# A fused GFNet and GEGLU kernel: the first piece of the forward matrix issued from ScalarE's DMA queue

## Chip, cores and metric

The kernel runs on 1 core of one Trainium2 chip. The metric is the device time in microseconds (us) of one execution. The runs of the kernel before lie between 456.63 and 457.2 us, with a median of 457.14 us over 3 runs.

## What is computed

The input x has 2048 rows of 512 numbers, all float32. The first half of the reference normalises each row, takes a two-dimensional real FFT, multiplies by complex weights, transforms back and adds x. The second half normalises the result again and runs a gated feed-forward layer with 1376 hidden columns, and adds its input.

```python
X = rfft2(layernorm(x));  X = X * (w_r + 1j * w_i);  h = x + irfft2(X)
n = layernorm(h)
g = n @ w_gate;  u = n @ w_up
h2 = h + (gelu(g) * u) @ w_down
```

## The kernel before, in words

**Tiling.** The FFTs are written as matrix products with cosine and sine tables, in stages. The 2048 rows are held as 128 partitions times 16 blocks: `gh[:, b]` is block b of x (128 x 512), and the forward matrix `mfs` holds for each block b a 128 x 128 piece `mfs[:, b]`. The prediction is about the first stage, the transform over the rows, which takes the first 33 of some 455 us. The stages behind it are the transform over the columns with the filter (lines 411 to 482), the way back, and the feed-forward layer with its products split in three (line 96) for precision, which is most of the span.

**One block of the first stage.** For each block b:

- VectorE (DVE) takes mean and variance: `stats` (line 220) and `merge` (line 223). For blocks 5, 7, 9, 11 and 13 ScalarE (ACT) does that instead: `mean` (line 228) and `square` (line 233).
- `root` (line 240) takes 1/sqrt on ACT, with line 241 beside it on DVE, and `newton` (lines 246 to 248) refines it on DVE. The result is `rs[:, b]`.
- `fold` (lines 262 and 263) is on GpSimd (POOL): sums and differences of the two halves of a row, written to `pn`. `fold2` (lines 275 to 277) is a second difference on DVE, written to `uv`.
- `scale` (line 256) on ACT multiplies `mfs[:, b]` by `rs[:, b]` and writes `ms`. So a block needs its piece of the forward matrix here and nowhere else, and the layernorm's scale is folded into the matrix.
- `transform` (line 288) is the product on TensorE (PE) of `pn` and `uv` with `ms`; `keep` (line 293) moves the result from PSUM to `ts` on ACT.

From block 2 on blocks go in pairs (`GROUPS`, line 28), except the last two. Lines 298 to 398 write the order of all these steps out by hand; each engine executes its own instructions strictly in that order, so an instruction that waits holds up everything behind it on its engine.

**Loads.** All DMAs of the kernel before are issued from SyncE (SP), in the order of the code. `load_x` (line 182) loads blocks of x, `load_m` (line 179) pieces of the forward matrix:

```python
act.activation(m4[:, :1], eps, AF.Abs_reciprocal_sqrt)   # L184: loads ACT's table early
load_x(0, 1)
load_x(1, 2)
load_m(0, 2)      # the line that changes: 128 KB
load_x(2, 4)
load_x(4, 6)
load_m(2, 8)
```

A load of one block of x is 256 KB, of two blocks 512 KB. Behind these come the rest of x, the rest of the matrix, small tables (line 196), and weights (lines 131, 132, 202 and on). Completion of the DMAs is counted on eight semaphores that the loads take in turn, so the ninth load of the program waits at issue for the first one to land, the tenth for the second, and so on.

Of the kernel before, what the change touches and what calls it, by code (L numbers as in the profile page):

```python
# [57 lines left out]
def kernel(  # L58
# [15 lines left out]
    nc = tc.nc  # L74
# [87 lines left out]
    with (  # L162
# [8 lines left out]
        mfs = w1.tile([P, NB, P], F32, name="mfs", bufs=1)  # L171
# [6 lines left out]
        def load_m(b0, b1):  # L178
            nc.sync.dma_start(mfs[:, b0:b1], mf[:, b0:b1])

        def load_x(b0, b1):
            nc.sync.dma_start(gh[:, b0:b1], x3[:, b0:b1])
# [1 line left out]
        act.activation(m4[:, :1], eps, AF.Abs_reciprocal_sqrt)  # L184
        load_x(0, 1)
        load_x(1, 2)
        load_m(0, 2)
        load_x(2, 4)
        load_x(4, 6)
        load_m(2, 8)  # L190
# [965 lines left out]
```

## Time and profile before

| what | value |
|---|---|
| runs of the kernel before, median (lowest to highest) | 457.14 us (456.63 to 457.2), 3 runs |
| the profiled execution's own time | 456.41 us |
| span of its trace, first to last instruction | 454.6 us |
| time outside the span | 1.81 us |
| busy share of PE, DVE, ACT, POOL | 97%, 61%, 45%, 61% |
| DMA: moved in the span | 41.05 MB |

Every timestamp below counts from the first instruction of the span. A row of the timeline gives start, duration, engine, line, operation, what is written and read, how many instructions are merged in the row, and in brackets the idle time of the engine ahead of it and what ended it. SPq is SyncE's queue of DMA issues: the duration of its row is that of the issue, and the data land later. PEld is the loading of weights into TensorE.

### The profile page before, as it was taken

To read this page: it belongs to the slowest core of one execution; us is meant where nothing else is said; L and a number is where in the kernel's file an instruction comes from. 1 tells how busy PE (TensorE), PEld (TensorE's weight loads), DVE (VectorE), ACT (ScalarE), POOL (GpSimd) and SP (SyncE) were. 2 spreads that over 40 slices of the span, in tenths; PEclk is the share of its full clock that TensorE was granted. 3 is DMA by queue.
4 is the path that set the end of the run, shared out by engine and by line. 5 is a ranking of instruction groups with operands and counts; after the bars stand their busy time and mean duration, and the time that the engine had idled before them with its cause. 6 is when DMAs were issued, how large, how long until landed. Compare 5 with 4: busy or idle time off the path is not lost.

```text
span 454.6 us, 6435 instructions
## 1 busy us (share of the span) xinstructions
PE 438.9 (97%) x2289; PEld 371.4 (82%) x2289; DVE 276.9 (61%) x513; ACT 206.6 (45%) x433; POOL 275.5 (61%) x305
## 2 busy tenths in 40 slices
PE   3999998999999999999999999999999999999997
PEld 3899998788967777887888888888888888888876
DVE  5966986797665676358744579256565355535453
ACT  3979876688751233024422776242243024302420
POOL 5985996968868578828752744155566536663210
PEclk9999999999999999999999999999999999999999
DMA  8994804300031122112210203131022102210013
GB/s 253 399 406 132 284 32 156 123 25 1 25 115 47 48 92 92 48 47 71 69 46 25 70 25 128 57 85 55 25 70 69 48 24 71 69 46 25 23 66 121
DMA packets 21168, 41.05 MB, mean 90 GB/s; under 512 B 2064, under 2 KB 7696, under 8 KB 21008
## 3 DMA queue, kind: packets, MB, share of 16 engines
q1 hardware_dynamic: 21136, 40.64, 26.2%
q8 instruction: 18, 0.29, 0.3%
q14 instruction: 14, 0.11, 0.1%
HBM read 36.44 MB, written 4.19 MB: 89 GB/s over the span
## 4 chain that ended last, share of the span: by engine, by line
PE 89%; ACT 4%; DVE 2%; DMA 2%; issue 1%; SPq 1%; DVEq 0%; ACTq 0%
PE ps L747 26%; PE ps L100 15%; PE ps L102 15%; PE ps L101 15%; PE ps L416 3%; PE ps L515 3%; PE ps L427 3%; PE ps L448 2%; PE ps L288 2%; DMA gh<-in_x 2%; PE ps L848 1%; PE ps L956 1%; PE ps L554 1%; ACT ts L293 1%; PE ps L548 1%
## 5 line engine op out<-in xcount | busy, mean ns | idle before, releaser
L100 PE MATMUL ps<-cb,gu 128*128 128x512 f32 (+1 forms) x336 | 127.8, 380 | 2.0 <-ACT s L651 1.6
L747 PE MATMUL ps<-wd,a 128*128 128x512 f32 (+1 forms) x537 | 126.1, 388 | 0.2 <-DVE gh L750 0.2
L102 PE MATMUL ps<-cb,gu 128*128 128x512 f32 (+1 forms) x336 | 124.9, 372 | 0.0
L101 PE MATMUL ps<-cb,gu 128*128 128x512 f32 (+1 forms) x336 | 124.8, 371 | 0.0
L747 PEld LDWEIGHTS ps<-wd,a 128*128 128x128 f32 x537 | 99.2, 188 | 22.4 <-DVE gh L957 0.9
L156 POOL TENSOR_TENSOR gu<-raw,gu 128x768 fp32r<-128x768 f32 (+1 forms) x54 | 78.2, 1476 | 40.0 <-DVE gu L153 38.7
L651 ACT ACTIVATE s<-ps 128x512 f32<-128x512 f32 (+1 forms) x72 | 40.4, 561 | 134.4 <-PE ps L102 134.2
L100 PEld LDWEIGHTS ps<-cb,gu 128*128 128x128 f32 x336 | 63.2, 188 | 15.0 <-ACT s L651 2.2
L101 PEld LDWEIGHTS ps<-cb,gu 128*128 128x128 f32 x336 | 63.2, 188 | 11.7 <-issue 1.0
L102 PEld LDWEIGHTS ps<-cb,gu 128*128 128x128 f32 x336 | 63.2, 188 | 11.1
L753 DVE TENSOR_TENSOR gh<-ps,gh 128x512 f32<-128x512 f32 x48 | 33.0, 690 | 53.5 <-PE ps L747 53.4
L496 POOL TENSOR_TENSOR wd<-wdr,wd 128x512 fp32r<-128x512 f32 x22 | 28.5, 1295 | 51.5 <-ACT wd L494 51.5
L660 DVE TENSOR_TENSOR ps<-ps,s 128x512 f32<-128x512 f32 (+1 forms) x48 | 31.0, 649 | 24.8 <-PE ps L102 22.5
L666 ACT ACTIVATE a<-ps 128x512 fp32r<-128x512 f32 (+1 forms) x48 | 26.9, 561 | 39.0 <-DVE ps L660 38.6
L673 DVE TENSOR_TENSOR a<-ps,a 128x512 fp32r<-128x512 f32 (+1 forms) x48 | 30.7, 640 | 11.8 <-ACT a L666 10.4
L138 POOL TENSOR_TENSOR raw<-raw 128x256 f32<-128x256 f32 x20 | 14.7, 737 | 37.8 <-DMA raw<-in_wgu 36.7
L654 DVE TENSOR_TENSOR s<-ps,s 128x512 f32<-128x512 f32 (+1 forms) x48 | 30.8, 642 | 10.3 <-PE ps L102 8.7
L657 ACT ACTIVATE s<-s 128x512 f32<-128x512 f32 (+1 forms) x48 | 28.2, 592 | 18.4 <-DVE s L654 18.4
L654 DVE TENSOR_TENSOR ps<-ps,s 128x512 f32<-128x512 f32 (+1 forms) x24 | 15.7, 654 | 27.7 <-ACT s L651 27.7
L288 PE MATMUL ps<-ms,pn 128*128 128x128 f32 x120 | 17.6, 297 | 8.3 <-ACT ms L256 8.1
L288 PEld LDWEIGHTS ps<-ms,pn 128*128 128x128 f32 x120 | 16.1, 210 | 8.8 <-POOL pn L263 8.8
L153 DVE CAST gu<-raw 128x1792 fp32r<-128x1792 f32 x18 | 19.6, 1091 | 4.5 <-PE ps L101 2.9
(124 smaller groups left out, 609.7 us busy)
## 6 DMA issues: line engine op xcount, KB each, us to landing
raw<-in_wgu SPq DMA_DIRECT2D x40, 256.0 KB, 3.1
wt<-in_w SPq DMA_DIRECT2D x16, 520.0 KB, 5.4
wdr<-in_wd SPq DMA_DIRECT2D x22, 256.0 KB, 2.6
out<-gh SPq DMA_DIRECT2D x15, 256.0 KB, 2.0
gh<-in_x SPq DMA_DIRECT2D x7, 512.0 KB, 9.6
row<-in_x SPq DMA_DIRECT2D x12, 256.0 KB, 3.0
mis<-in_mi SPq DMA_DIRECT2D x1, 1024.0 KB, 10.7
a<-in_x SPq DMA_DIRECT2D x4, 256.0 KB, 4.3
```

The lines of the kernel that those rows point to most:

```text
L100: pe.matmul(o, lh, rh, start=(i == 0 and not onto), stop=False, skip_group_check=True)
L101: pe.matmul(o, lh, rl, start=False, stop=False, skip_group_check=True)
L102: last = pe.matmul(o, ll, rh, start=False, stop=(i == n - 1), skip_group_check=True)
L156: pooled["lo"] = pool.tensor_tensor(r[:, 1, m], t[:, m], r[:, 0, m].bitcast(F32), op=ALU.subtract)
L288: pe.matmul(pt[:, c], o, mc, start=(z == 0), stop=(z == len(parts[b][c]) - 1))
L496: pool.tensor_tensor(r[:, 1], t, r[:, 0].bitcast(F32), op=ALU.subtract)
L651: return lambda: act.activation(to, a, AF.Copy)
L654: return lambda: dve.tensor_tensor(to, a, b, op=ALU.add)
L660: return lambda: dve.tensor_tensor(u, u, g, op=ALU.mult)
L673: dve.tensor_tensor(a[:, 1], u, a[:, 0].bitcast(F32), op=ALU.subtract)
L747: pe.matmul(o, parts_of[tiles.index((q, f))][:, ha, i // 4, r], wds[f][:, hw, c], start=start, stop=stop)
L753: dve.tensor_tensor(gh[:, b, c], o, gh[:, b, c], op=ALU.add)
```

## The change

One line is replaced. The 128 KB piece of the forward matrix for blocks 0 and 1 is issued by ScalarE instead of SyncE. All other loads stay on SyncE in their order.

```diff
         act.activation(m4[:, :1], eps, AF.Abs_reciprocal_sqrt)
         load_x(0, 1)
         load_x(1, 2)
-        load_m(0, 2)
+        nc.scalar.dma_start(mfs[:, :2], mf[:, :2])
         load_x(2, 4)
         load_x(4, 6)
         load_m(2, 8)
```

On SyncE the first loads of the program stood as follows before; `gh` is x, `mfs` the forward matrix, and L196 loads the first small table.

```order
L182 DMA gh<-in_x 128x512 x2
L179 DMA mfs<-in_mf 128x256
L182 DMA gh<-in_x 128x1024 x2
L179 DMA mfs<-in_mf 128x768
L182 DMA gh<-in_x 128x1024 x2
L179 DMA mfs<-in_mf 128x1024
L182 DMA gh<-in_x 128x1024 x3
L196 DMA dfs<-in_df 128x520
```

And on SyncE in the changed program:

```order
L182 DMA gh<-in_x 128x512 x2
L182 DMA gh<-in_x 128x1024 x2
L179 DMA mfs<-in_mf 128x768
L182 DMA gh<-in_x 128x1024 x2
L179 DMA mfs<-in_mf 128x1024
L182 DMA gh<-in_x 128x1024 x3
L196 DMA dfs<-in_df 128x520
```

The row of 128x256 is gone, and every load behind it stands one place further ahead.

On ScalarE the changed program begins with these rows; `m` is the scrap output of the first activation, `ms` the scaled matrix, `jk` a scrap output of the statistics.

```order
L187 DMA mfs<-in_mf 128x256
L184 ACT_TABLE_LOAD
L184 ACTIVATE m_98<-eps 128x1
L240 ACTIVATE rs<-mv,eps 128x1
L256 ACTIVATE ms<-mfs,rs 128x128
L240 ACTIVATE rs<-mv,eps 128x1
L256 ACTIVATE ms<-mfs,rs 128x128
L228 ACTIVATE jk,m_98<-gh 128x512
```

The first row is new; the seven others stood there before in this order. The DMA stands ahead of the table load and of the first activation, though the code has it behind that activation. TensorE, VectorE and GpSimd have the same rows as before.

## Prediction

> **What bounds the kernel now.** I read the page first.
>
> ```profile
> span 454.6 us, 6435 instructions
> PE 438.9 (97%) x2289; PEld 371.4 (82%) x2289; DVE 276.9 (61%) x513; ACT 206.6 (45%) x433; POOL 275.5 (61%) x305
> ```
>
> TensorE is busy for 97% of the span, so the kernel is TensorE's work plus whatever keeps TensorE from beginning it. A load at the front can only change the second part. So next I read the chain of work that ended last, in order of time, for the first 30 us.
>
> ```profile
> 1.63 0.42 SPq L179
> 2.10 0.43 SPq L182
> ...
> 3.52 8.86 DMA gh<-in_x
> 12.38 0.02 issue
> 12.40 0.03 ACT jk L228
> ...
> 22.10 0.14 issue
> 22.23 7.83 PE ps L288 x68
> ```
>
> Three stretches follow each other: SyncE's issues, one load of x (blocks 6 and 7) that takes 8.86 us from issue to landing, and ScalarE's work, until TensorE takes over at 22.23 us and keeps the chain. The matrix piece that the change moves is in this chain only as an issue of 0.42 us at 1.63; its data are not in it. Now the timelines of the engines, ScalarE first.
>
> ```profile
> 0.73 1.28 ACT L184 ACT_TABLE_LOAD   x1 [0.73 <-PEq L1147]
> 2.02 0.20 ACT L184 ACTIVATE m<-eps 128x1 f32<-128x1 f32 x1
> 4.46 0.29 ACT L240 ACTIVATE rs<-mv,eps 128x1 f32<-128x1 f32 x1 [2.24 <-DVE mv L223]
> 6.75 0.40 ACT L256 ACTIVATE ms<-mfs,rs 128x128 f32<-128x128 f32 x1 [1.99 <-DMA mfs<-in_mf]
> 7.06 0.28 ACT L240 ACTIVATE rs<-mv,eps 128x1 f32<-128x1 f32 x1
> 7.96 0.40 ACT L256 ACTIVATE ms<-mfs,rs 128x128 f32<-128x128 f32 x1 [0.63 <-DVE rs L248]
> 9.94 0.63 ACT L228 ACTIVATE jk<-gh 128x512 f32<-128x512 f32 x1 [1.58 <-DMA gh<-in_x]
> ...
> 12.40 0.63 ACT L228 ACTIVATE jk<-gh 128x512 f32<-128x512 f32 x1 [0.22 <-DMA gh<-in_x]
> ```
>
> At 6.75 ScalarE has waited 1.99 us for the piece in question. But at 9.94 it waits again, 1.58 us, for blocks 4 and 5 of x, and at 12.40 another 0.22 us for blocks 6 and 7. GpSimd and TensorE:
>
> ```profile
> 5.62 0.72 POOL L263 TENSOR_TENSOR pn<-gh 128x256 f32<-128x256 f32 x1
> 8.28 1.27 POOL L262 TENSOR_TENSOR pn<-gh 128x512 f32<-128x512 f32 x1 [1.94 <-DMA gh<-in_x]
> ```
>
> ```profile
> 7.29 2.05 PE L288 MATMUL ps<-ms,pn 128*128 128x128 f32 x8 [7.29 <-ACT ms L256]
> ...
> 9.99 1.92 PE L288 MATMUL ps<-ms,pn 128*128 128x128 f32 x8
> 11.69 1.06 PE L288 MATMUL ps<-ms,uv 128*128 128x128 f32 x4
> 13.56 2.02 PE L288 MATMUL ps<-ms,pn 128*128 128x128 f32 x16 [0.80 <-ACT ms L256]
> ...
> 16.31 1.06 PE L288 MATMUL ps<-ms,pn 128*128 128x128 f32 x8
> 17.20 0.61 PE L288 MATMUL ps<-ms,uv 128*128 128x128 f32 x4
> ```
>
> GpSimd waits 1.94 us for blocks 2 and 3 of x, at 8.28. TensorE begins at 7.29 when the scaled matrix is there, does blocks 0 and 1, stops for 0.80 us and begins block 2 at 13.56. Weight loading shows who paces TensorE after that.
>
> ```profile
> 19.15 0.97 PEld L288 LDWEIGHTS ps<-ms,pn 128*128 128x128 f32 x8 [0.18 <-POOL pn L263]
> 22.20 0.97 PEld L288 LDWEIGHTS ps<-ms,pn 128*128 128x128 f32 x8 [0.30 <-POOL pn L263]
> ```
>
> So the front has two pacemakers of nearly the same length: GpSimd from 8.28 on, released by blocks 2 and 3, and ScalarE from 9.94 on, released by blocks 4 and 5 and once more by 6 and 7. The dense region moves only if **all these landings of x** move; blocks 0 and 1 are done in front of it and cost nothing when they end sooner.
>
> **The change, part by part.**
>
> *Matrix piece sooner.* Landing times by issue, in the first 30 us:
>
> ```profile
> gh<-in_x SPq DMA_DIRECT2D x2, 256.0 KB, 2.9
> mfs<-in_mf SPq DMA_DIRECT2D x1, 128.0 KB, 5.0
> ```
>
> Before, the piece is issued at 1.63 and lands 5.0 us later, at 6.63. After, its issue is ScalarE's first row, at about 0.73; with the 2.9 us of the first x loads it lands near 3.6, with its own 5.0 us near 5.7. The scale `rs` of block 0 decides then. DVE rows:
>
> ```profile
> 3.52 0.69 DVE L220 BATCH_NORM_STATS2 bn<-gh 128x6 f32<-128x512 f32 x1 [2.66 <-DMA gh<-in_x]
> 5.52 0.16 DVE L248 SCALAR_TENSOR_TENSOR rs<-ps,rs 128x1 f32<-128x1 f32 x1
> 7.37 0.16 DVE L246 SCALAR_TENSOR_TENSOR ps<-rs,ps 128x1 f32<-128x1 f32 x1 [0.75 <-ACT rs L240]
> ```
>
> It is ready at 5.52 + 0.16 = 5.68, so ScalarE scales at 5.7 to 6.1 instead of 6.75, and TensorE starts at 6.3 to 6.7 instead of 7.29. DVE's wait of 0.75 us at 7.37 mostly goes too, as ScalarE's second root is no longer held behind the scaling. What is late next is x: ScalarE's 1.58 us wait, GpSimd's 1.94 and TensorE's 0.80 simply grow. Worth **0** of the end.
>
> *One issue less on SyncE.* Blocks 2 and 3 are issued at 1.63 instead of 2.10, and each load behind them 2.10 - 1.63 = 0.47 us earlier. If their landings followed, the gain would be 0.47. But the same 128 KB still go through the same DMA engines, ahead of them or beside. How full these are:
>
> ```profile
> 1.50:2.00 0.50, 0.00 (x0) 0.00 (x0) 0.00 (x0) 0.50 (x1) 0.00 (x0) 1.00 0.40 66
> 2.00:2.50 0.50, 0.00 (x0) 0.00 (x0) 0.00 (x0) 0.22 (x2) 0.00 (x0) 1.00 0.83 250
> ...
> 3.00:3.50 0.50, 0.00 (x0) 0.00 (x0) 0.00 (x0) 0.00 (x0) 0.00 (x0) 1.00 0.97 363
> ...
> 9.00:9.50 0.50, 0.50 (x4) 0.50 (x4) 0.50 (x2) 0.00 (x0) 0.50 (x1) 1.00 1.06 285
> ...
> 11.50:12.00 0.50, 0.50 (x4) 0.50 (x4) 0.23 (x2) 0.50 (x3) 0.50 (x2) 1.00 1.08 442
> ```
>
> The last two columns are the DMA engines' share and GB/s. From 1.5 to 2.5 us they are free for (1 - 0.40) x 0.5 + (1 - 0.83) x 0.5 = 0.39 us; later they are full. The piece needs 131 KB / 363 GB/s = 0.36 us. If it goes wholly into that free time, all x loads behind it land up to 0.36 us sooner; if the two queues share whatever makes the descriptors, nothing is won, and the time is spent ahead of x. So 0 to 0.36 from the bytes, 0.47 from the issues; below nothing, 0.36 lost if block 0 is pushed back and no free time is used. I take **0.3 gained**, since the free time is there in the rows and the piece fits.
>
> The Trainium skill (DMA: Bandwidth & Descriptors, "Issuing engines are not separate DMA queues") says that issues from several engines run on the same DMA engines, interleave, and save only the sequencer's issue time. By it the gain is the issue alone, so the sum would be the 0.47 of the rows at most and no bandwidth. The trace of before has one data queue, so no run yet shows the sharing.
>
> *Block 0 of x shares the engines.* It may land up to 0.36 us after 3.52, its share with the piece. Everything up to GpSimd's fold of block 1 (ends 5.62 + 0.72 = 6.34) then moves by that, and is still ahead of 8.28. DVE has lost a 0.75 us wait, so it is not late either. Worth 0; the cover is the wait for blocks 2 and 3.
>
> *ScalarE's issue.* It stands ahead of the table load. SyncE's issue takes 0.42 here; even with 1.5 us the first activation would end at 2.02 + 0.20 + 1.5 = 3.7, and the next instruction is needed at 4.46 (2.24 us idle ahead of it). Worth 0; without that cover, the issue's 0.42. Behind the new DMA stand the table load and every activation, and nobody asks for them before 4.46.
>
> *Semaphores.* The first load of the program is now this piece, so the ninth, matrix pieces 8 to 15, waits at issue for it instead of block 0 of x. Even if it lands as late as 5.7 us, the loads in between (four of 512 KB and one of 384 KB) keep the DMA engines busy; at 363 GB/s they take over 6 us. Worth 0.
>
> **Sum.** The profiled execution took 456.41 us, 454.6 of it span. 456.41 - 0.3 = 456.1. The median shown is 457.14, 0.73 above the profiled one; against it the forecast is **456.8 us**. From 22.23 us the shift is passed on whole, as no later wait of TensorE is for a DMA in the list of waits; the largest is
>
> ```profile
> PE ps L100 <- ACT s L651: 1.6, 3, 0.7
> ```
>
> **The rivals.**
>
> *A. The slow start of x goes away (faster).* Blocks 2 and 3 take from 2.10 to 8.28, though 0.5 MB at 442 GB/s are 1.2 us; the rates from 4 to 9.5 us are near 285 GB/s with the engines full, and 442 later. If mixing the matrix rows between x loads is what slows them, they speed up when it is gone. Then GpSimd can start at 6.34 (1.94 sooner) and ScalarE 1.58 sooner; the smaller one holds: 457.14 - 1.6 = 455.5. Against: the slow stretch lasts to 9.5, long after the piece of 128 KB is through.
>
> *B. TensorE's slow matmuls reach into block 2 (slower).* Its eight matmuls from 9.99 to 11.69 take 0.21 each, the eight from 16.31 to 17.20 take 0.11, of one shape. Something makes TensorE fast only between 11.69 and 13.56, in or near the 0.80 us pause. If it counts recent work, an earlier start (by 0.6 to 1.0) with a longer pause behind it (up to 1.8) may put this off into block 2. A delay of w in dense work costs half of w, less the 0.18 + 0.30 = 0.48 that TensorE waits for GpSimd later; it decides from w = 1.0 us on. With w = 3.4 us it costs 1.7 - 0.48 = 1.2, less 0.3 gained 0.9: 457.14 + 0.9 = 458.0. At the worst all 24 matmuls of blocks 2 and 3 are slow, 24 x 0.10 - 0.48 - 0.3 = 1.6: 458.7. For it: before, the speed came just in time. Against: an earlier start may as well bring it earlier.
>
> The Trainium skill (TensorE: Matmul & The Clock Gate, "Part 1: The HAM clock gate") has a free-running window of about 3.4 us that must be busy before the clock doubles. The doubling agrees with 0.21 and 0.11; the granted clock of the profile stands at 1.00 in all rows above, so it does not show it. By this rule the point moves from run to run.
>
> *C. The piece is not sooner.* Its own 5.0 us recur on the second queue and no x load gains: 457.1.
>
> **How the numbers follow.** Forecast (0 to 0.5 gained) 0.46, A 0.25, B 0.22, C 0.07. About 0.2%, 0.9 us, is what a measurement of this kernel can tell from no change. Faster by more: A and a tail of the forecast, 0.27. Slower by more: the two thirds of B in which the speed comes 3.4 us late or later, 0.15. Within: 0.58. The range takes in A and the middle of B, 455.4 to 458.1, and leaves out the worst of B; the forecast's own is 456.6 to 457.2.
>
> **What will show it.** ScalarE's row of line 256 at 5.7 to 6.1 and no wait for `mfs`: the first step. GpSimd's row now at 8.28, ScalarE's now at 9.94 and 12.40 each about 0.3 earlier: the sum. If GpSimd starts near 6.3, A. If matmuls of block 2 still take 0.21, B. I am wrong if these three rows move by over 0.5 us, or if they move and the end does not follow.

## Result and the profile after

| | before | after |
|---|---|---|
| median, same chip | 456.63 us (456.38 to 457.36), 7 runs | 455.19 us (454.97 to 456.28), 7 runs |
| ratio (95% interval) | | 0.9968 (0.9957 to 0.998) |
| profiled execution, its span | 456.41, 454.6 us | 455.09, 453.3 us |

The changed kernel is about 0.3% faster; the forecast of 456.8 was 1.6 us too high. Of that, 0.5 us is the kernel before itself, whose median was 457.14 in the three runs ahead of the prediction and is 456.63 in the seven here. First the rows that were to show the matrix piece. ScalarE's timeline after the change (ACTq is its queue of DMA issues):

```profile
0.73 0.40 ACTq L187 DMA_DIRECT2D mfs<-in_mf  x1
1.16 1.28 ACT L184 ACT_TABLE_LOAD   x1 [1.16 <-PEq L1147]
...
5.20 0.29 ACT L240 ACTIVATE rs<-mv,eps 128x1 f32<-128x1 f32 x1 [2.54 <-DVE mv L223]
...
6.90 0.40 ACT L256 ACTIVATE ms<-mfs,rs 128x128 f32<-128x128 f32 x1 [1.40 <-DVE rs L248]
...
8.41 0.61 ACT L228 ACTIVATE jk<-gh 128x512 f32<-128x512 f32 x1
...
11.21 0.62 ACT L228 ACTIVATE jk<-gh 128x512 f32<-128x512 f32 x1
```

The scaling at 6.90 no longer waits for the piece but for DVE's `rs`, and begins later than before (6.75). The two statistics rows of line 228 have lost their waits for x and come 1.5 and 1.2 us sooner. DVE, after, shows what holds `rs`:

```profile
4.25 0.69 DVE L220 BATCH_NORM_STATS2 bn<-gh 128x6 f32<-128x512 f32 x1 [3.39 <-DMA gh<-in_x]
...
5.71 0.69 DVE L220 BATCH_NORM_STATS2 bn<-gh 128x6 f32<-128x512 f32 x1 [0.35 <-DMA gh<-in_x]
...
6.70 0.16 DVE L248 SCALAR_TENSOR_TENSOR rs<-ps,rs 128x1 f32<-128x1 f32 x1
```

Block 0 of x comes 0.73 us later (4.25 against 3.52), and DVE now waits for block 1 too. Those second statistics stand ahead of block 0's `newton`, so `rs` is ready at 6.86 instead of 5.68. GpSimd and TensorE after:

```profile
4.30 0.72 POOL L262 TENSOR_TENSOR pn<-gh 128x256 f32<-128x256 f32 x1 [3.00 <-DMA gh<-in_x]
...
7.14 1.46 POOL L262 TENSOR_TENSOR pn<-gh 128x512 f32<-128x512 f32 x1
```

```profile
7.44 2.04 PE L288 MATMUL ps<-ms,pn 128*128 128x128 f32 x8 [7.44 <-ACT ms L256]
...
11.66 0.61 PE L288 MATMUL ps<-ms,uv 128*128 128x128 f32 x4
12.36 2.02 PE L288 MATMUL ps<-ms,pn 128*128 128x128 f32 x16
...
32.40 2.95 PE L416 MATMUL ps<-dfs,ts 128*128 128x130 f32 x24 [0.69 <-ACT ts L293]
```

GpSimd's fold of blocks 2 and 3 begins at 7.14 instead of 8.28 and waits for nothing: it follows the fold ahead of it. TensorE starts 0.15 later, yet begins block 2 at 12.36 instead of 13.56, its pause of 0.80 us gone. The next stage's first row before was:

```profile
33.43 2.95 PE L416 MATMUL ps<-dfs,ts 128*128 128x130 f32 x24 [0.69 <-ACT ts L293]
```

So 33.43 - 32.40 = 1.03 us of the span's 1.3 are won in the first stage. The other 0.3 lies behind that point, and there the spans of this study's profiles scatter by more: 420.8 to 422.9 us from this row on, 421.2 before and 420.9 after. What holds the front after the change is the chain of work that ended last, in order of time:

```profile
1.16 4.53 DMA gh<-in_x
...
6.90 0.41 ACT ms L256
7.31 0.14 issue
7.44 4.83 PE ps L288 x24
12.27 0.08 issue
12.36 8.62 PE ps L288 x72
```

The load in it is now block 1 of x, landed at 5.69, and no longer blocks 6 and 7; TensorE keeps the chain from 7.44 on instead of from 22.23.

Where the 1.03 came from is in the DMA columns. Windows (length, busy times, granted clock, DMA share, GB/s), before and then after:

```profile
1.50:4.00 2.50, 0.00 (x0) 0.00 (x0) 0.48 (x1) 0.72 (x2) 0.43 (x1) 1.00 0.81 259
4.00:9.50 5.50, 2.21 (x10) 2.24 (x11) 4.48 (x17) 1.28 (x4) 3.56 (x5) 1.00 0.96 274
```

```profile
1.50:4.00 2.50, 0.00 (x0) 0.00 (x0) 0.00 (x0) 1.15 (x2) 0.00 (x0) 1.00 0.82 184
4.00:9.50 5.50, 2.06 (x10) 2.09 (x11) 4.60 (x15) 2.24 (x7) 5.15 (x6) 1.00 1.02 381
```

The first loads are slower (184 against 259 GB/s), and then the slow stretch that stood from 4 to 9.5 us is not there: 381 against 274, at nearly the same share. And these engines are as full at 274 as at 381, so fullness did not tell how fast they were.

### The profile page after: what moved, and what is told of

Its sections match the earlier page's. It is cut to its first block, busy times and chain, and to the rows that moved or that the text cites. A ratio compares the mean times of both kernels' runs of the same rounds, so it can differ in the third digit from the quotient of the medians.

```text
span 453.3 us, 6435 instructions
## 1 busy us (share of the span) xinstructions
PE 438.1 (97%) x2289; PEld 371.2 (82%) x2289; DVE 276.7 (61%) x513; ACT 206.5 (46%) x433; POOL 276.0 (61%) x305
## 4 chain that ended last, share of the span: by engine, by line
PE 93%; DVE 3%; ACT 2%; DMA 1%; issue 1%; SPq 0%; DVEq 0%
PE ps L747 26%; PE ps L100 15%; PE ps L102 15%; PE ps L101 15%; PE ps L288 5%; PE ps L416 3%; PE ps L515 3%; PE ps L427 3%; PE ps L448 2%; PE ps L848 1%; PE ps L956 1%; DMA gh<-in_x 1%; PE ps L554 1%; PE ps L548 1%; PE ps L845 0%
```

## Experiments

In the table, "fold 0" and "fold 2" are the starts of GpSimd's folds of block 0 and of blocks 2 and 3, "x 4, 5" is when the first instruction released by blocks 4 and 5 begins, and GB/s is the rate from 4 to 9.5 us, all of the profiled execution. "Clock" counts the runs whose mean granted clock is at or below 0.9975; half the clock for 3.4 us takes 1.7 us of 455 away and gives 0.996. The kernel before has medians of 457.55, 457.04, 457.22, 457.31 and 457.54 us in the five batches (19 to 31 runs each), and the ratios on record are to its runs on the same chip; they are not the quotients of these medians (e6's 0.9955 would be 0.9974). The capital names in the expectations are theories, told where they fall or hold. Where every engine but SP has to keep its order for a comparison, ScalarE's order in the first stage was written out by hand as in the kernel before (all but e1, e3, e4, e8); in e9, e15 and e18 TensorE still interleaves blocks 2 and 3 a little differently.

| kernel | median us | ratio (95%) | clock | fold 0 | fold 2 | x 4, 5 | GB/s |
|---|---|---|---|---|---|---|---|
| before | | | 57 of 132 | 3.57 | 8.28 | 9.94 | 274 |
| after | 455.19 | 0.9968 (0.9957 to 0.998) | 0 of 7 | 4.30 | 7.14 | 8.33 | 381 |
| e1 before again | 457.49 | 0.9999 (0.9977 to 1.0021) | 3 of 10 | 3.87 | 9.09 | 10.26 | 279 |
| e2 first on SyncE | 456.84 | 0.9977 (0.9953 to 1.0002) | 2 of 10 | 4.35 | 7.36 | 8.82 | 304 |
| e3 behind activation | 456.09 | 0.9968 (0.9946 to 0.999) | 0 of 10 | 3.83 | 7.71 | 8.87 | 330 |
| e4 x on ScalarE | 455.56 | 0.9954 (0.9936 to 0.9972) | 0 of 10 | 4.58 | 7.30 | 8.27 | 353 |
| e5 fourth on SyncE | 456.67 | 0.999 (0.9967 to 1.0013) | 0 of 10 | 3.59 | 6.89 | 9.56 | 280 |
| e6 another piece third | 455.83 | 0.9955 (0.9938 to 0.9972) | 0 of 10 | 4.43 | 7.19 | 8.66 | 323 |
| e7 newton first | 455.95 | 0.9973 (0.9954 to 0.9992) | 0 of 10 | 4.31 | 7.74 | 8.94 | 364 |
| e8 after again | 455.39 | 0.997 (0.9945 to 0.9995) | 1 of 10 | 4.22 | 7.05 | 8.24 | 366 |
| e9 table, 128 KB, early | 456.86 | 0.9982 (0.9964 to 1.0001) | 3 of 10 | 4.11 | 8.89 | 10.24 | 284 |
| e10 table, 128 KB, late | 457.49 | 1.0013 (0.9987 to 1.0039) | 7 of 10 | 3.79 | 9.60 | 10.81 | 257 |
| e11 half the piece | 457.07 | 0.9989 (0.997 to 1.0009) | 6 of 10 | 3.89 | 8.47 | 9.67 | 267 |
| e12 alternate | 455.41 | 0.996 (0.9937 to 0.9983) | 0 of 7 | 4.55 | 8.51 | 7.15 | 367 |
| e13 start at block 1 | 457.25 | 1.0004 (0.9987 to 1.002) | 3 of 10 | 4.33 | 8.54 | 9.73 | 286 |
| e14 start at blocks 2, 3 | 460.12 | 1.005 (1.0031 to 1.0069) | 0 of 4 | 8.70 | 11.43 | 9.80 | 284 |
| e15 busy pause | 457.44 | 0.999 (0.9973 to 1.0008) | 0 of 12 | 3.78 | 9.59 | 10.79 | 267 |
| e16 two on ScalarE | 455.44 | 0.9955 (0.9938 to 0.9973) | 0 of 4 | 4.13 | 6.85 | 7.89 | 328 |
| e17 swapped | 456.07 | 0.997 (0.9949 to 0.9991) | 0 of 10 | 4.42 | 7.46 | 8.70 | 345 |
| e18 table, 256 KB, early | 455.98 | 0.9969 (0.995 to 0.9988) | 0 of 10 | 4.53 | 7.59 | 8.97 | 333 |

(x 4, 5 of e12 is the landing itself.)

**Is it chance, and does the place of the piece on SyncE decide?** e1 is the unchanged kernel before, e8 the unchanged kernel after.

> The kernel before, unchanged, profiled once more. Three theories of why the loads of x behind the first two became faster. PLACE: the matrix piece standing between loads of x on SyncE's queue makes the x loads behind it slow (285 GB/s from 4 to 9.5 us). START: two queues at the start load both at once, slow the first loads and put the DMA engines out of step, and the later loads then run without stalls. CHANCE: the slow stretch comes and goes from one execution to the next, and one profile of each kernel is one draw. PLACE and START: GpSimd's first fold of a pair starts at 8.0 to 8.5 us again, ratio 0.999 to 1.001. CHANCE: it starts anywhere from 7.0 to 8.5, and times spread by over 1 us.

> The changed kernel, unchanged, profiled once more on the chip of this batch, as the measure for the three others. If the fast loads belong to the change: first fold of a pair at 7.0 to 7.7, ratio 0.996 to 0.998. If the one profile was luck: 8.0 or more.

The slow stretch is there again in e1, and gone again in e8. GpSimd and the window in e1:

```profile
9.09 1.27 POOL L262 TENSOR_TENSOR pn<-gh 128x512 f32<-128x512 f32 x1 [2.45 <-DMA gh<-in_x]
```

```profile
4.00:9.50 5.50, 1.71 (x8) 1.74 (x9) 4.03 (x15) 1.28 (x4) 3.05 (x5) 1.00 0.86 279
```

So it belongs to the kernel. Four edits place the piece elsewhere, or send another load to ScalarE. e2:

```diff
+        load_m(0, 2)
         load_x(0, 1)
         load_x(1, 2)
-        load_m(0, 2)
```

> One queue only: the matrix piece is issued first on SyncE, ahead of x; all other orders as in the kernel before. PLACE: no matrix rows stand between the first four loads of x, so GpSimd's first fold of a pair starts at 7.0 to 7.5 and the ratio is near 0.997. START: one queue, engines in step, so the slow stretch is there again: 8.2 to 8.5, ratio 0.999 to 1.001. CHANCE: either, independent of the edit.

With one queue and nothing between the first four x loads, e2 lies between the two kernels (304 GB/s), and its interval holds no change. But its fold of blocks 2 and 3, at 7.36, is where PLACE had it and not START, and the next stage begins as early as in e3 (32.76), which has two queues:

```profile
32.66 2.95 PE L416 MATMUL ps<-dfs,ts 128*128 128x130 f32 x24 [0.69 <-ACT ts L293]
```

e3 keeps ScalarE but means to issue later:

```diff
-        act.activation(m4[:, :1], eps, AF.Abs_reciprocal_sqrt)
+        warm = act.activation(m4[:, :1], eps, AF.Abs_reciprocal_sqrt)
...
-        load_m(0, 2)
+        with tc.issue_after(warm.ins): nc.scalar.dma_start(mfs[:, :2], mf[:, :2])
```

> The piece on ScalarE's queue, but held behind the first activation, so that it is issued at about 2.2 us (before: 1.63 on SyncE) and the two first loads of x have the DMA engines alone. PLACE: x loads stay fast as in the changed kernel, the fold of the first pair starts at 6.5 to 7.2, and block 0 lands at 3.5 as before; ratio 0.996 to 0.998. START: the first loads go in step, so the slow stretch returns: 8.0 to 8.4, ratio 0.999 to 1.001.

The gain is that of the change, but it did not test what it was for: the issue came at 0.90, not behind the activation.

```profile
0.73 1.28 ACT L184 ACT_TABLE_LOAD   x1 [0.73 <-PEq L1147]
0.90 0.37 ACTq L187 DMA_DIRECT2D mfs<-in_mf  x1
2.03 0.20 ACT L184 ACTIVATE m<-eps 128x1 f32<-128x1 f32 x1
```

e4 leaves the piece in its place on SyncE, between x loads, and moves block 1 of x instead:

```diff
-        load_x(1, 2)
+        nc.scalar.dma_start(gh[:, 1:2], x3[:, 1:2])
         load_m(0, 2)
```

> The piece stays third in the program on SyncE, between loads of x; block 1 of x goes to ScalarE's queue instead, issued first there. PLACE: matrix rows still stand between x loads on SyncE, so the slow stretch is there: fold of the first pair at 7.8 to 8.4, ratio 0.999 to 1.001. START: two queues at the start, so the slow stretch is gone: 6.8 to 7.3, ratio near 0.997.

```profile
4.00:9.50 5.50, 2.23 (x10) 2.27 (x11) 4.73 (x15) 2.22 (x7) 4.92 (x6) 1.00 1.01 353
```

All the gain is there although the piece was not touched. So the piece between the x loads does not slow them where a load of 256 KB runs on the second queue. Whether it does with one queue, as e2 suggests, e4 does not tell.

**SyncE's third place, or the early start of TensorE?** e5 puts the piece fourth, behind blocks 2 and 3; e6 is the changed kernel with other 128 KB in the third place:

```diff
-        load_m(0, 2)
         load_x(2, 4)
+        load_m(0, 2)
```

> One queue only: the piece is issued fourth on SyncE, behind blocks 2 and 3 of x, which are so issued at 1.63 as in the changed kernel. Three theories now. START: two queues at the start take the stalls of the first loads side by side, and the later loads run through. SLOT: what counts is that blocks 2 and 3 of x are issued one slot earlier on SyncE, so that the DMA engines do not run short at 3.5 to 4.5 us (share 0.81 and 0.72 before). PLACE: matrix rows between loads of x slow those behind. START: GpSimd's first fold of a pair at 8.0 to 9.1 as before. SLOT: at 7.0 to 7.5, blocks 4 and 5 near 8.5. PLACE: blocks 2 and 3 early (below 7), blocks 4 and 5 slow (near 10). In all of them the first scaling waits for the piece until 5.5 to 7, so the ratio says little: 0.997 to 1.001.

```diff
-        load_m(0, 2)
-        load_x(2, 4)
+        nc.scalar.dma_start(mfs[:, :2], mf[:, :2])
+        load_m(2, 4); load_x(2, 4)
         load_x(4, 6)
-        load_m(2, 8)
+        load_m(4, 8)
```

> The changed kernel, and a second 128 KB piece (matrix blocks 2 and 3, cut from the load of blocks 2 to 7) put back in the third slot on SyncE. So two queues at the start, but the third slot is used up as before. START: first fold of a pair at 7.0 to 7.7, ratio 0.996 to 0.998 as for the changed kernel. SLOT and PLACE: slow stretch again, 8.0 to 9.1, ratio 0.999 to 1.001.

SyncE's first table load is issued when blocks 4 and 5 have landed. In e5, then e6:

```profile
9.56 0.33 SPq L196 DMA_DIRECT2D dfs<-in_df  x1
```

```profile
8.66 0.33 SPq L196 DMA_DIRECT2D dfs<-in_df  x1
```

With the third place free (e5), blocks 2 and 3 come sooner, but the slow stretch then catches blocks 4 and 5, which is what PLACE expected. With it taken (e6) the gain stays, so SLOT falls, and PLACE again does not hold with two queues. e7 is the changed kernel with block 0's `newton` ahead of block 1's statistics on DVE, so that TensorE does start early:

```diff
             root(0, 1)
+            newton(0, 1)
+            scale(0)
             stats(1)
-            newton(0, 1)
             merge(1)
             root(1, 1)
             fold2(0, 1)
-            scale(0)
```

> The changed kernel with one more edit: on VectorE the statistics of block 1 stand behind the refinement of block 0's scale instead of ahead of it. In the changed kernel TensorE starts at 7.44 and works without a pause over 0.1 us from then on; its start waits for block 1 of x through these statistics. If TensorE's start now sets the end, it starts at 6.4 to 6.7 and the kernel is up to 0.9 us faster than the changed one (ratio to before 0.994 to 0.996). If GpSimd's and ScalarE's pace behind blocks 2 to 7 of x sets the end, the pause ahead of block 2 grows and nothing is gained (0.996 to 0.998).

```profile
6.67 2.05 PE L288 MATMUL ps<-ms,pn 128*128 128x128 f32 x8 [6.67 <-ACT ms L256]
...
12.76 2.02 PE L288 MATMUL ps<-ms,pn 128*128 128x128 f32 x16 [0.64 <-ACT ms L256]
```

TensorE starts at 6.67, waits 0.64 us again ahead of block 2, and nothing is gained beside e8. Blocks 2 to 5 of x came later in this profile, too (fold 2 at 7.74 waits for its load), so it does not tell what an earlier start would be worth with x as early as in e8.

**What must the second queue carry, and when?** e9 loads half of a table that is needed far later (`cis`, 128 KB) from ScalarE at the start and leaves all else as before; e10 does it, with the same second edit, behind block 0's root.

```diff
-        load_x(0, 1)
+        load_x(0, 1); nc.scalar.dma_start(cis[:, 0], ci[:, 0])
...
-        for c, a in ((dfs, df), (cfs, cf), (cis, ci)):
+        for c, a in ((dfs, df), (cfs, cf), (cis[:, 1], ci[:, 1])):
```

> SyncE's first nine loads exactly as in the kernel before, the piece third among them. ScalarE's queue gets an unrelated 128 KB at the start: half of a small table that is needed near 47 us. (TensorE interleaves blocks 2 and 3 a little differently.) START: two queues at the start, so blocks 4 and 5 of x land at 8.2 to 8.9 although nothing of the changed line is changed and 128 KB more are ahead; ratio 0.996 to 0.998. If it is the moved piece itself: slow stretch as before, blocks 4 and 5 near 10, ratio 0.999 to 1.002.

```diff
-            root(0, 1)
+            root(0, 1); nc.scalar.dma_start(cis[:, 0], ci[:, 0])
```

> The same unrelated 128 KB on ScalarE's queue, but behind its first root, which waits for VectorE until 4.5 us. START: one queue until 4.5 us, so the slow stretch is there as before: blocks 4 and 5 of x at 9.2 to 10.3, ratio 0.999 to 1.001. If any use of a second queue is enough, or the program's having one: as the changed kernel, 8.2 to 8.9, ratio 0.996 to 0.998.

In e9 blocks 4 and 5 landed as late as in the kernel before:

```profile
10.24 0.33 SPq L196 DMA_DIRECT2D dfs<-in_df  x1
```

So an early start on the second queue is not enough by itself, and START as stated falls. e10, issued at 4.70, did not help either. e11 sends only block 0's 64 KB of the piece by ScalarE:

```diff
-        load_x(0, 1)
+        load_x(0, 1); nc.scalar.dma_start(mfs[:, :1], mf[:, :1])
...
-        load_m(0, 2)
+        load_m(1, 2)
```

> Half the dose: only block 0's part of the piece (64 KB) goes first on ScalarE's queue; block 1's 64 KB stay third on SyncE. START: the gain is there or half of it, blocks 4 and 5 at 8.2 to 9.3, ratio 0.996 to 0.999. If the full 128 KB must be gone from SyncE: near 10, ratio 0.999 to 1.001.

Slow stretch, no gain. e17 exchanges the piece with the next one of equal size, blocks 2 and 3's; e18 takes the whole table (256 KB) on ScalarE, all else on SyncE:

```diff
-        load_x(0, 1)
+        load_x(0, 1); nc.scalar.dma_start(mfs[:, 2:4], mf[:, 2:4])
...
-        load_m(2, 8)
+        load_m(4, 8)
```

> As the run with another piece third, but with the two pieces of the matrix changed over: the piece of blocks 0 and 1 stays third on SyncE as before, and ScalarE's queue gets blocks 2 and 3 (128 KB) at the start. Two theories are left. ROWS: a load on the second queue at the start helps if its rows lie far apart in memory (those of the matrix 8 KB, those of x 32 KB), and not if they lie close together (the table, 2 KB). BYTES: it helps if it brings enough bytes. ROWS: blocks 4 and 5 of x land at 8.2 to 9.0, ratio 0.9945 to 0.997. BYTES has 128 KB here, as with the table, which did not help: 9.6 to 10.3, ratio 0.998 to 1.000.

```diff
-        load_x(0, 1)
+        load_x(0, 1); nc.scalar.dma_start(cis, ci)
...
-        for c, a in ((dfs, df), (cfs, cf), (cis, ci)):
+        for c, a in ((dfs, df), (cfs, cf)):
```

> All first loads on SyncE as before, the piece third; ScalarE's queue gets the whole small table (256 KB, one stretch of memory) at the start. ROWS: it lies close together, so the slow stretch stays: blocks 4 and 5 at 9.6 to 10.8, ratio 0.998 to 1.001. BYTES: 256 KB, as block 1 of x on that queue, which helped: 8.2 to 9.0, ratio 0.9945 to 0.998.

Their windows, e17 and e18:

```profile
4.00:9.50 5.50, 2.38 (x11) 2.42 (x12) 4.89 (x15) 2.04 (x7) 4.81 (x6) 1.00 1.02 345
```

```profile
4.00:9.50 5.50, 2.28 (x11) 2.31 (x12) 4.78 (x15) 1.81 (x5) 4.68 (x6) 1.00 1.02 333
```

Neither has the slow stretch. As far as one profile of each can tell, a load of either array will do, if there is enough of it: 128 KB of matrix or 256 KB of table, but not 64 KB of matrix or 128 KB of table. Neither bytes alone (e17 against e9) nor the kind of data alone (e18) decides, so BYTES and ROWS both fall as stated. Two kernels with more on ScalarE, e12 (block 1 and blocks 4 and 5) and e16 (block 1 and the piece), looked for a better version:

```diff
-        load_x(1, 2)
+        nc.scalar.dma_start(gh[:, 1:2], x3[:, 1:2])
...
-        load_x(4, 6)
+        nc.scalar.dma_start(gh[:, 4:6], x3[:, 4:6])
```

> A version that might beat both: block 1 of x, and blocks 4 and 5, go to ScalarE's queue at the start, the rest stays on SyncE with the piece second. START: the early loads run side by side still more; blocks 4 and 5 land at 7.5 to 8.5 and the ratio is 0.994 to 0.997. Against it: block 0 and the pair of blocks 2 and 3, which are wanted first, share the DMA engines with them and land later (above 4.5 and 7.5), and the ratio is 0.997 to 1.000.

```diff
-        load_x(1, 2)
-        load_m(0, 2)
+        nc.scalar.dma_start(gh[:, 1:2], x3[:, 1:2])
+        nc.scalar.dma_start(mfs[:, :2], mf[:, :2])
```

> A version that might beat both: block 1 of x and the piece both go to ScalarE's queue, so SyncE has block 0 and at once blocks 2 and 3. If the slow stretch is away as in the kernels with block 1 or the piece on ScalarE's queue: blocks 2 and 3 land at 6.3 to 7.1, ratio 0.994 to 0.997. If the piece, now behind block 1 of x, or block 0 lands too late (above 5.5 and 4.7), TensorE starts after 7.5 and the ratio is 0.997 to 0.999.

x lands earlier still in e16 (7.89), but the times, 455.41 and 455.44, are those of the changed kernel: from 6.85 (GpSimd) and 8.23 (ScalarE) on the engines of e16 follow their own work, not x.

**Is it the engines' work that slows the loads?** In nine of the ten profiles without the slow stretch the engines begin at 4.13 or later, before at 3.57. e13 and e14 let block 0's fold and statistics of the kernel before wait for a later load as well:

```diff
-        load_x(1, 2)
+        first = load_x(1, 2)        # e14: first = load_x(2, 4)
...
-            dve.bn_stats(bns[b], gh[:, b])
+            i = dve.bn_stats(bns[b], gh[:, b]); behind(i, first) if b == 0 else None
```

> The kernel before with all loads as they were; only the first fold of GpSimd and the first statistics of VectorE also wait for block 1 of x, so they start at 4.2 to 4.5 instead of 3.6 to 3.9. In the runs so far the slow stretch came in every kernel whose compute began before 4.15 us but one, and in none that began later. COMPUTE: the early reading by GpSimd and VectorE while the loads still write is what slows the loads: blocks 4 and 5 of x land at 8.2 to 8.9, ratio 0.996 to 0.999. FIRST LOADS: an early landing of block 0 and the slow stretch have a common cause in the loads themselves, and compute has no part in it: blocks 4 and 5 at 9.5 to 10.8, ratio 0.999 to 1.003.

> As before, but GpSimd and VectorE wait for blocks 2 and 3 of x as well, so that nothing but the loads runs until these have landed. COMPUTE: with no compute beside them the loads run through: blocks 2 and 3 land at 6 to 7.1, blocks 4 and 5 at 8 to 8.9. FIRST LOADS: the slow stretch is there all the same: 7.3 to 9.5 and 9.5 to 10.8. The time is longer by 1 to 4 us either way, since the first blocks start late.

```profile
4.00:9.50 5.50, 0.00 (x0) 0.00 (x0) 0.81 (x2) 0.00 (x0) 0.80 (x2) 1.00 0.91 284
```

In e14 nothing but the loads runs until 8.66, and they still go at 284 GB/s; e13 has 286. COMPUTE falls: the slow stretch is made among the transfers.

**Rival B's clock.** e10's profile has one long pause of TensorE, and behind it (TensorE's windows: length, busy time, granted clock, DMA share, GB/s):

```profile
14.59 2.69 PE L288 MATMUL ps<-ms,pn 128*128 128x128 f32 x11 [3.09 <-POOL pn L263]
```

```profile
12.00:14.00 2.00, 0.00 (x0) 0.98 1.03 422
14.00:16.00 2.00, 1.41 (x6) 0.50 1.03 414
...
18.00:20.00 2.00, 2.00 (x11) 0.50 1.06 376
20.00:22.00 2.00, 2.00 (x17) 0.82 1.08 383
22.00:24.00 2.00, 2.00 (x21) 1.00 1.03 404
```

The granted clock falls to half in the pause; worked out from the windows, from 13.9 to 20.7 us, some 6.8 us. 11 matmuls fit into 2 us where 21 do later. In e11's profile the clock falls behind a pause of 2.05 us (11.48 to 13.53), for 3.4 us:

```profile
14.00:16.00 2.00, 2.00 (x12) 0.54 1.04 426
16.00:18.00 2.00, 2.00 (x13) 0.61 1.01 400
```

By these windows it falls at 14.2, 0.6 us after the matmuls have begun again. e15 gives TensorE four extra matmul calls into an idle bank (a product that nothing reads) behind block 1, so that its work lasts longer into the pause:

```diff
-            transform(1)
+            transform(1); [pe.matmul(ps[:, 6, :P], parts[1][0][0], mss[1], start=True, stop=True) for _ in range(4)]
```

> The kernel before with four more matmul calls of TensorE behind block 1, into a bank not yet in use, to fill its pause ahead of block 2; the loads are as before. In 35 of 90 runs of the kernel before the mean granted clock is 0.997 or less, and these runs are 1.0 us longer at the median; of the changed kernel 1 in 17. CLOCK: the pause ahead of block 2 lets the clock drop to 0.50 for 3.4 us or more, so filling it takes these runs away: at most 1 in 10 with a clock of 0.997 or less, and the median is 0.2 to 0.8 us shorter although the slow stretch stays (ratio 0.998 to 0.9995). If the clock drops for another reason: 3 to 5 in 10 again, ratio 1.000 to 1.003.

```profile
10.83 1.06 PE L311 MATMUL ps<-ms,pn 128*128 128x128 f32 x8
14.20 1.35 PE L288 MATMUL ps<-ms,pn 128*128 128x128 f32 x10 [2.31 <-ACT ms L256]
```

x is as slow as before and a pause of 2.31 us remains, but no run of 12 has the drop, where 57 of 132 of the kernel before have a clock as low. So TensorE's work ahead of the pause has a part in the drop, and CLOCK holds that far. That the length of the pause decides is not shown: 2.31 us is longer than e11's 2.05, and e3 has a pause of 1.05 us in its profile and a low clock in none of 10 runs. The worth of the drop in time is not resolved by e15 (0.9973 to 1.0008), since the extra products cost something too. 3.4 and 6.8 us are one and two of the windows that the Trainium skill (TensorE: Matmul & The Clock Gate, "Part 1: The HAM clock gate") gives.

## Why the prediction was wrong

- **"One issue less on SyncE … I take 0.3 gained"** is the step that failed: its size. 1.4 us came between the medians, 1.03 of it at line 416 in the two profiles (e1 and e8, on other chips, stand 33.95 - 32.20 = 1.75 apart there). I priced the free time of the DMA engines and the 0.47 us of the issue and took the rate of the loads as given. The rate is what changed, 274 to 381 GB/s over 5.5 us. The rows I quoted showed it as open: engines full at 285 GB/s and later full at 442.
- **Rival A** had nearly the time (455.5) and the right place, GpSimd's fold of blocks 2 and 3 and ScalarE's waits. Whether it had the cause is open, because the change does two things at once: it takes the matrix rows out from between the x loads, and it starts a second queue. The second does it without the first: e4, e6, e17 and e18 keep matrix rows between the x loads, and the slow stretch is gone. The first does much of it without the second: e2 wins 0.77 of the 1.03 us at line 416, in one profile and with a time that is not clear of no change. All nine profiles with blocks 4 and 5 at 9.56 us or later have the piece, or half of it (e11), between x loads on SyncE, and those of them with a second queue at the start have the smallest loads of their kind on it (e9, e11). The ten others with a second queue at the start have blocks 4 and 5 by 8.97 us. Of the eight with one queue at the start, seven are at 9.56 to 10.81 and e2 at 8.82.
- **The rule of the Trainium skill** (DMA: Bandwidth & Descriptors, "Issuing engines are not separate DMA queues"), by which only issue time is saved, differs from the measurement: e6 saves SyncE no issue ahead of blocks 2 and 3 and gains 0.45% (0.28 to 0.62).
- **"Matrix piece sooner"**: the piece landed in 3.7 us, at 4.4, but TensorE did not start at 6.3 to 6.7: 7.44. I held DVE's `rs` at 5.68, though the `stats` of block 1 stand ahead of it and block 1 came later. For its worth of 0 speaks e7, where TensorE started at 6.67 and nothing was gained.
- **"Block 0 of x shares the engines"**: 0.73 later, not up to 0.36. The worth of 0 is not shown. Its cover, GpSimd's wait for blocks 2 and 3, is gone: the fold at 7.14 follows the fold ahead of it, and the chain of the changed kernel starts from block 1 of x. What an earlier landing of blocks 0 and 1 would bring was not measured apart from the rest.
- **ScalarE's issue and the semaphores** were worth 0 as said: 0.40 us, all in front of a wait of 2.54.
- **Rival B** was turned round: where the pause of TensorE goes, a low clock nearly goes too (1 of the 17 runs of after and e8); the kernel before has it in 43% of its runs. That this is the drop seen in e10 and e11 is inferred from the mean clock, since neither profile of the kernel before caught one. Runs of before with the low clock have a median of 457.75 us, those without 456.81. So some 0.43 x 0.94 = 0.4 us of a mean may be a second gain, not in my sum; part of it can be a later landing of x in the same runs. Without low clocks on either side, 456.81 against 455.34 (16 of the 17 runs, other chips in part) leaves 1.5 for x; on e8's chip alone, 456.44 (17 runs) against 455.36 (9 runs), it is 1.1.
- **The passing on** held: the dense region moved with the front, and the 1.03 us at line 416 are there at the end.

What stays open is why the loads slow down on one queue. It is not chance (e1, e8), SyncE's third slot (e6) nor the engines' work (e14). The place of the matrix rows does no harm where the second queue carries enough (e4, e6), but with one queue e2 and e5 came out as PLACE expected, so which of the two effects of the change works in the changed kernel is open. In nine of the ten profiles without it block 0 of x lands late (fold 0 at 4.13 or behind, before 3.57); e2, with one queue, fits this too (4.35). But e3 at 3.83 is an exception, and e9 has the slow stretch at 4.11, so this does not settle it. How packets of two queues interleave within a DMA engine was not tried.

## What to carry to other kernels

Where DMA engines are full and the rate is far below what they reach later, the rate is the quantity to forecast, and a second queue at the start is a cheap trial, and so is the order on the first one. Try them apart, since one line can change both. Give the second queue enough (here 128 KB of one array did and 128 KB of another did not), and expect the very first load to land later. The gain ends where the engines' own work takes over from the landings. Look at the granted clock of many runs, not of one profile: a pause between the first matmuls may cost half the clock in some runs only.

## What was not expected of the hardware

A DMA queued behind an activation on ScalarE need not wait for it: in e3 it was issued at 0.90 us, while the table load (0.73 to 2.01) still ran. Behind an activation that itself waits on a semaphore it does, as in e10, 0.01 us after that one began:

```profile
4.69 0.29 ACT L240 ACTIVATE rs<-mv,eps 128x1 f32<-128x1 f32 x1 [2.46 <-DVE mv L223]
...
4.70 0.38 ACTq L300 DMA_DIRECT2D cis<-in_ci  x1
```
